# Two linear-attention and MLP layers on one core: entry sums, scalings, reciprocals and statistics rearranged

## The chip, the core and the metric

The kernel runs on one core of a Trainium2 chip. The core has five engines that run on their own and meet at semaphores: TensorE (PE; its weight loads are shown as PEld), VectorE (DVE), ScalarE (ACT), GpSimd (POOL) and SyncE (SP), which here issues all DMAs. The metric is the time of one execution on the device in microseconds. The kernel before takes 752.74 us (median of three runs, 752.65 to 752.99).

## The reference

The input x is 2048 rows of 576. Two blocks alternate, attention, MLP, attention, MLP, with the same weights both times, each behind a layer norm without gain, each added to x. Cut to what matters:

```python
q, k, v = ...                                # x @ wqkv, 32 heads of 18
phi = lambda t: where(t > 0, t + 1, exp(t)) + 1e-6
pq, pk = phi(q), phi(k)
kv  = einsum("bhsd,bhse->bhde", pk, v)       # per head, summed over all rows
z   = einsum("bhsd->bhd", pk)
num = einsum("bhqd,bhde->bhqe", pq, kv)
den = einsum("bhqd,bhd->bhq", pq, z)
x   = x + (num / den) @ wo
...
x   = x + gelu(layernorm(x) @ w1 + b1) @ w2 + b2    # 576 -> 4608 -> 576
```

## The kernel before

A row tile is 128 rows of x, so there are 16; a chunk is four row tiles. "Layer 0" and "layer 2" are the attentions, 1 and 3 the MLPs. The order of the work on each engine comes from three things: the order in which the program writes it, edges that only fix an order (`add_manual_dep` with NOSYNC; for TensorE they chain all its matmuls as written), and a planner at compile time that, where neither binds, puts on an engine what it reckons ready, the earlier written first. So ScalarE, VectorE and GpSimd may have an order other than the written one; each engine then runs its queue strictly in that order.

**Attention.** Instead of values, the kernel sums normalized rows against keys over all rows (`rows_by_keys`, matmuls L796) and multiplies the result by the value weights later (`kv_groups`, L849). Keys come in two halves of the heads. The first half's sums run during the row loop. The second half's are left for the entry, the stretch between the loop and the output stage: `sums(n)` does n row tiles of them, four matmuls of 0.12 us each (and one earlier for the tail). After the last one the sums are evicted to `k2` (`plus_eps`, L773 or L777), two by ScalarE and two by VectorE. Queries are projected feature group by feature group (`q_proj`, L718, L723) and passed through phi: an exponential (L640) and an identity (L644) on ScalarE, then L650 and the maximum L652 on VectorE. Four of the 18 query projections lie in the entry.

Denominators are computed for two chunks at a time (`den_stage`, L930; logarithm L934 and exponential L935 give reciprocals). `quad_stage` (L950) spreads the reciprocals of the last, small group of heads over a diagonal; `scale_stage` (L960, L962, L963) multiplies with them. For the four full groups `quarter_stage(c)` spreads them by 16 small matmuls (L974) into all four banks of the PSUM pool `ps_h` and ScalarE copies each bank out (L978); `quarter_scale(c, groups, after)` multiplies the queries in place on VectorE (L984), one instruction per group. `kv_groups` is masked on VectorE (L862) into block-diagonal `kvT`, and `kv_wo_half` (L878) multiplies it by half of the output weights. For the small group VectorE evicts (L881) and GpSimd copies the rows on (L884); the others are evicted by ScalarE or VectorE (L890). All of q, kv, kvwo, spread reciprocals and transposes share the four banks of `ps_h`, so a matmul that opens a bank waits for an eviction.

The output stage takes row tiles t = 0 to 15 in turn: ten matmuls (`wo_products`, L1121) into one of two other PSUM buffers, the residual sum on VectorE (L694), the store.

**Layer norm.** `LNPipe` carries each row tile through stages, one stage per `tick`: statistics (on VectorE L455, L456, L462 and L473 or L476; or on ScalarE in two passes, L429 for the mean and L442 for the squares, then L448 on GpSimd), the power -1/2 on GpSimd (L491), mean times that (L499), the normalization (L505 or L526 on GpSimd), and a transposition: by TensorE (L568) with a copy by ScalarE (L574), or by DMA from SyncE's queue (L552, L557), where it stands in one chain with the loads of the MLP's weights (L291). `hold` lets ticks pass first; `tp_at` is the output tile before which the transposition is not issued. In layer 0, `BY_ACT` names the input tiles whose statistics ScalarE takes; after each output stage the first four row tiles of the sum enter the pipe for the MLP.

## Time and profile before

The profiled execution took 753.01 us on the device; its span, from the first to the last instruction, is 751.3 us, at a granted TensorE clock of 1.00.

| stretch, us | what runs | PE busy | DVE busy | ACT busy | POOL busy |
|---|---|---|---|---|---|
| 0 to 20 | loads, first keys of layer 0 | 18.16 | 15.62 | 11.58 | 9.53 |
| 20 to 36 | layer 0, row loop | 15.63 | 12.32 | 12.11 | 13.38 |
| 36 to 55 | layer 0, row loop | 18.90 | 11.69 | 11.38 | 7.29 |
| 55 to 66 | layer 0, entry | 10.95 | 7.62 | 7.53 | 0.00 |
| 66 to 76 | layer 0, entry | 9.84 | 7.58 | 7.23 | 2.63 |
| 76 to 97 | layer 0, output stage | 21.00 | 17.41 | 10.84 | 9.15 |
| 378 to 424 | layer 2, row loop | 45.74 | 33.29 | 32.71 | 2.03 |
| 424 to 434 | layer 2, entry | 9.95 | 4.44 | 5.51 | 0.00 |
| 434 to 445 | layer 2, entry | 10.72 | 8.21 | 7.34 | 1.69 |
| 445 to 467 | layer 2, output stage | 21.49 | 16.60 | 12.40 | 8.64 |

The MLPs (97 to 378 and 467 to 751) keep TensorE busy throughout. A row of a timeline has the start in us, the time taken, the engine, the line, the operation, what it writes from what it reads, the shapes and the number of instructions merged; in brackets stands how long the engine idled before it and what ended that. A merged row can hide short waits, because the end of a matmul is modelled: the distance between starts shows them.

### The profile page before, as it was taken

The page shows a single profiled execution, that of the slowest core. Times are in us where ns is not written, and L with a number is a line of the kernel's source. Part 1 is how long each engine was busy: PE and PEld are TensorE (multiplying, and loading weights), DVE is VectorE, ACT ScalarE, POOL GpSimd, SP SyncE. Part 2 cuts the span into 40 slices and gives each one's busy share as a digit, 9 for nine tenths or more (in the row PEclk, how much of TensorE's full clock was granted, in tenths as well). Part 3 has the DMA queues.
Part 4 walks back from the last instruction along what each step waited for, and adds up shares of the span by engine and source line. Part 5 has one row for each costly group of instructions (what it writes and reads, how often), then busy time and mean ns, then how long its engine had stood idle before and what let it go on. Part 6 is the DMA issues. An engine that isn't in the chain of part 4 may idle for free.

```text
span 751.3 us, 15670 instructions
## 1 busy us (share of the span) xinstructions
PE 744.3 (99%) x6522; PEld 474.6 (63%) x6536; DVE 260.4 (35%) x645; ACT 314.8 (42%) x703; POOL 118.6 (16%) x220
## 2 busy tenths in 40 slices
PE   9999999999999999999999999999999999999998
PEld 5666744774576467547776666457646754774476
DVE  7767824235034404301367576500330041000000
ACT  5766656007501740363057665650263046105600
POOL 4831402003011201301000013300120020002000
PEclk9999999999999999999999999999999999999999
DMA  7797993027213701411404248420330033011000
GB/s 186 205 224 195 262 356 84 33 72 192 66 41 108 182 23 48 127 48 32 130 22 120 53 131 308 138 58 17 126 85 1 28 116 84 9 32 56 2 16 17
DMA packets 88545, 75.72 MB, mean 101 GB/s; under 512 B 45002, under 2 KB 73114, under 8 KB 88474
## 3 DMA queue, kind: packets, MB, share of 16 engines
q1 hardware_dynamic: 88474, 74.72, 35.0%
q8 instruction: 51, 0.84, 0.5%
q14 instruction: 20, 0.16, 0.1%
HBM read 48.10 MB, written 24.77 MB: 97 GB/s over the span
## 4 chain that ended last, share of the span: by engine, by line
PE 95%; DMA 2%; ACT 1%; SPq 1%; issue 1%; POOL 0%; DVE 0%; POOLq 0%
PE m_ps L1300 37%; PE h_ps L1236 21%; PE hp_ps L1236 17%; PE wo_ps L1121 5%; PE k_ps L751 4%; PE q_ps L718 4%; PE k_ps L796 4%; PE m_half L1300 1%; DMA wqkv_sb<-in_A_wqkv_dram 1%; PE q_ps L723 1%; DMA yT<-x 1%; PE k_tail L796 0%; PE rden_ps L974 0%; ACT turned L978 0%; PE kvwo_half L878 0%
## 5 line engine op out<-in xcount | busy, mean ns | idle before, releaser
L1300 PE MATMUL m_ps<-w_sb,hT 128*128 128x288 bf16 x2232 | 274.8, 286 | 0.0
L1300 PEld LDWEIGHTS <-hT 128*128 128x128 bf16 x2304 | 224.3, 98 | 60.4 <-issue 3.4
L1236 PEld LDWEIGHTS <-w_sb 64*128 64x128 bf16 x2304 | 124.6, 94 | 136.5 <-issue 1.9
L1236 PE MATMUL hp_ps<-yT,w_sb 64*128 64x512 bf16 x1152 | 178.0, 376 | 0.0
L1236 PE MATMUL h_ps<-yT,w_sb 64*128 64x512 bf16 x1152 | 147.9, 376 | 0.0
L1241 ACT COPY relay_sb<-relay_sb 128x1 f32<-128x1 f32 x144 | 28.5, 198 | 261.1 <-PE h_ps L1236 218.8
L1232 ACT ACTIVATE hT<-h_ps,b1T 128x512 bf16<-128x512 f32 x144 | 91.1, 683 | 44.4 <-PE h_ps L1236 44.4
L491 POOL TENSOR_TENSOR ln_rstd<-ln_u,neg_half 128x1 f32<-128x1 f32 x62 | 34.7, 561 | 367.2 <-DVE ln_u L473 213.1
L1232 ACT ACTIVATE hT<-hp_ps,b1T 128x512 bf16<-128x512 f32 x144 | 91.1, 692 | 0.0
L694 DVE TENSOR_TENSOR xbf<-m_ps,xo 128x576 bf16<-128x576 f32 x15 | 11.4, 758 | 213.5 <-PE m_ps L1300 213.5
L694 DVE TENSOR_TENSOR xo<-m_ps,xo 128x576 f32<-128x576 f32 x16 | 12.1, 758 | 167.8 <-PE m_ps L1300 167.8
L677 POOL TENSOR_TENSOR xo<-xo,b_bc 128x576 f32<-128x576 f32 x32 | 41.2, 1291 | 104.0 <-DMA xo<-x_d 91.4
L1236 PE MATMUL h_ps<-yT,w_tail 64*128 64x512 bf16 x144 | 54.1, 376 | 0.0
L1236 PE MATMUL hp_ps<-yT,w_tail 64*128 64x512 bf16 x144 | 54.1, 376 | 0.0
L751 PE MATMUL k_ps<-wqkv_sb,yT 128*128 128x288 bf16 (+1 forms) x320 | 44.5, 286 | 0.7 <-DMA wqkv_sb<-in_A_wqkv_dram 0.4
L1121 PE MATMUL wo_ps<-kvwo,pq 128*128 128x288 bf16 x320 | 42.3, 286 | 0.0
L718 PE MATMUL q_ps<-yT,wqkv_sb 128*128 128x512 bf16 x146 | 38.8, 379 | 0.7
L751 PEld LDWEIGHTS <-yT 128*128 128x128 bf16 x320 | 30.6, 97 | 11.8 <-DMA yT<-x 0.6
L1236 PEld LDWEIGHTS <-w_tail 64*128 64x128 bf16 x288 | 27.1, 94 | 17.1
L1121 PEld LDWEIGHTS <-pq 128*128 128x128 bf16 x320 | 30.6, 98 | 8.4 <-issue 0.3
L640 ACT ACTIVATE phi_e<-q_ps 128x512 bf16<-128x512 f32 (+1 forms) x38 | 21.6, 574 | 24.1 <-PE q_ps L718 21.1
L349 DVE STREAM_TRANSPOSE turned<-y_ring 128x576 bf16<-128x576 bf16 x40 | 30.4, 767 | 0.4
(161 smaller groups left out, 542.6 us busy)
## 6 DMA issues: line engine op xcount, KB each, us to landing
xo<-x_d SPq DMA_DIRECT2D x48, 288.0 KB
x_d<-xo SPq DMA_DIRECT2D x32, 288.0 KB
xl<-x_d SPq DMA_DIRECT2D x24, 288.0 KB
y_d<-turned SPq DMA_DIRECT2D x40, 144.0 KB
w_sb<-in_B_w_dram SPq DMA_DIRECT2D x6, 864.0 KB
yT<-y_d SPq DMA_DIRECT2D x10, 512.0 KB
w_sb<-in_B_w_dram SPq DMA_DIRECT2D x9, 512.0 KB
x_d<-xn SPq DMA_DIRECT2D x16, 288.0 KB
```

Of the source, the lines that this page charges most:

```text
L349: turn = nc.vector.transpose(out=turned[:, :, j, :], in_=y[:, 0:D])
L491: power = nc.gpsimd.tensor_tensor(out=rstd[:], in0=it["u"][:], in1=neg_half[:], op=ALU.pow)
L677: nc.gpsimd.tensor_tensor(out=xo[:], in0=xo[:], in1=b2_bc[:], op=ALU.add)
L694: total = nc.vector.tensor_tensor(out=xn[:, cols].rearrange("p (h n) -> p h n", h=2), in0=halves, in1=xo[:, cols].rearrange("p (h n) -> p ...
L718: pe(nc.tensor.matmul(qp[:], lhsT=wqkv_sb[:, k, g * P:(g + 1) * P], rhs=yT[:, k, c * CA:(c + 1) * CA], start=(k == 0), stop=(k == KD - 1)))
L751: pe(nc.tensor.matmul(kp[:, 0:n], lhsT=yT[:, k, t * P:(t + 1) * P], rhs=wqkv_sb[:, k, KH[half]:KH[half] + n], start=(k == 0), stop=(k == K ...
L796: pe(nc.tensor.matmul(dst, lhsT=lhsT, rhs=pk, start=(t == 0), stop=(t == NT - 1)))
L1121: pe(nc.tensor.matmul(wp[:, half, 0:HALF], lhsT=features, rhs=kvwo[slot][:, half * HALF:(half + 1) * HALF], start=(g == WO_ORDER[0]), stop ...
L1232: act_last["gelu"] = nc.scalar.activation(out=to, in_=ps, func=ACT.Gelu_apprx_tanh, bias=b1T[:, f:f + 1], scale=1.0).ins.name
L1236: mm = pe(nc.tensor.matmul(dst[n], lhsT=wt, rhs=mv, start=(seen[n] == 0), stop=(seen[n] == 8)))
L1241: relay = nc.scalar.copy(out=relay_sb[:, 1:2], in_=relay_sb[:, 0:1])
L1300: pe(nc.tensor.matmul(acc[half][:, 0:cols.stop - cols.start], lhsT=hT[f][:, j * P:(j + 1) * P], rhs=w2_sb[:, f, cols], start=(f == 0), sto ...
```

## The change

- Tile 10 of layer 0 leaves `BY_ACT`: VectorE takes its statistics. Its special ticks at t = 7 go.
- ScalarE takes the statistics of tile 3 of layer 0's sum (`t > 0` in place of `t in (1, 2)`). In layer 2, tile 2's second pass waits one tick more (`gap`) and is ordered behind the last scaling copy; for the input tiles the second pass loses its order edge.
- In the entry, a second row of sums stands ahead of `kv_wo_half(4, 0)`, and the query and the scalings of chunk 1 that stood in the middle go behind all sums and group 0's products. Scalings 0 and 1 follow there, ordered behind the eviction of the sums; scaling 2 behind the mask of groups 1 to 3; scaling 3 after output tile 1.
- `quad_stage(2)` runs on GpSimd after output tile 1, not on VectorE after tile 3.

```diff
-        BY_ACT = (10, 13)
+        BY_ACT = (13,)
...
-                        if it["t"] == BY_ACT[0] or it["kind"] == "B" and it["evac"] != "xbar":
-                            it["hold"] = int(it["kind"] == "A")
+                        if it["kind"] == "B" and it["evac"] != "xbar":
+                            it["hold"] = it["gap"]
                             continue
...
-                        if it["kind"] == "A":
-                            tc.add_manual_dep(two.ins, act_last["exp"], NOSYNC, reason="keys go on first")
+                        if it["gap"]:
+                            tc.add_manual_dep(two.ins, act_last["copy"], NOSYNC, reason="scalings first")
...
+                if engine is nc.vector:
+                    dve_last["k2"] = step.ins.name
...
-            def quad_stage(c, after=None):
+            def quad_stage(c):
...
-                    spread_out = nc.vector.tensor_tensor(
+                    spread_out = (nc.gpsimd if c else nc.vector).tensor_tensor(
...
-                    if t == 7:
-                        for _ in range(2):
-                            lnp.tick(transposes=0, only=BY_ACT[0])
...
             quarter_stage(1)
-            sums(1)
+            sums(2)
             kv_wo_half(4, 0)
             sums(1)
             kv_wo_half(4, 1)
-            quarter_scale(1, (0, 1, 2, 3), after=dve_last["quad"])
-            q_proj(*q_left.pop(0))
             sums(1)
             kv_wo_half(0, 0)
-            sums(1)
             kv_wo_half(0, 1)
+            quarter_scale(1, (0, 1), after=dve_last["k2"])
+            q_proj(*q_left.pop(0))
...
-                        hold, tp_at, by_act = ((2, 0, 4, 6)[t], (5, 7, 8, 12)[t], t in (1, 2))
+                        hold, tp_at, by_act = ((2, 0, 4, 6)[t], (5, 7, 8, 12)[t], t > 0)
...
             q_proj(*q_left.pop(0))
             kv_groups((1, 2, 3))
+            quarter_scale(1, (2,), after=dve_last["mask"])
             phi = q_proj(*q_left.pop(0), defer=True)
...
+                if t == 1:
+                    quarter_scale(1, (3,), after=total)
...
                 if t == 1:
                     den_stage(2)
-                if t == 3:
-                    quad_stage(2, after=total)
+                    quad_stage(2)
```

More of the change, by code (lines that the diff above doesn't have):

```diff
@@ L395, in __init__, with feed, tick @@
                 self.items = []
-            def feed(self, xt, t, kind, norm_eng, evac_eng="dve", load_from=None, after=None, hold=0, stats="dve", tp_at=0):
+            def feed(self, xt, t, kind, norm_eng, evac_eng="dve", load_from=None, after=None, hold=0, stats="dve", tp_at=0, gap=0):
                 self.items.append(dict(stage=(0 if load_from is None else -1), xt=xt, t=t, kind=kind,
                                        norm=norm_eng, evac=evac_eng, load=load_from,
-                                       after=after, hold=hold, stats=stats, tp_at=tp_at))
+                                       after=after, hold=hold, stats=stats, tp_at=tp_at, gap=gap))
             def busy(self):
                 return len(self.items)
-            def tick(self, transposes=1, only=None):
+            def tick(self, transposes=1):
                 land()
@@ L408, in tick @@
                     st = it["stage"]
-                    if only is not None and it["t"] != only:
-                        continue
                     if st == 4 and it["kind"] == "B" and it["evac"] == "xbar" and state["wo"] < it["tp_at"]:
@@ L865, in kv_groups @@
                     in1=maskz[0:126, :, :].unsqueeze(1).to_broadcast([126, n, 7, DH]), op=ALU.mult)
+                dve_last["mask"] = masked.ins.name
             def kv_wo_tiles():
@@ L945, in tile_of @@
                 return pq[(g, c - c % 2)][:, start:start + P], GF4 + j // 2
-            def quad_stage(c, after=None):
+            def quad_stage(c):
                 quad = blk.tile([P, D], BF16, name="quad_rden", tag="blk")
                 for i in range(2):
-                    spread_out = nc.vector.tensor_tensor(
+                    spread_out = (nc.gpsimd if c else nc.vector).tensor_tensor(
                         out=quad[:, 2 * i * P:2 * (i + 1) * P].rearrange("p (j n) -> p j n", j=2), in0=quad_mask[:],
                         in1=rden_of[c + i].unsqueeze(1).to_broadcast([P, 2, P]), op=ALU.mult)
-                    if after is not None:
-                        tc.add_manual_dep(spread_out.ins, after, NOSYNC, reason="sums first")
                 quad_rden[c] = quad
@@ L1130, in wo_stage @@
                     if li == 0:
-                        hold, tp_at, by_act = ((2, 0, 4, 6)[t], (5, 7, 8, 12)[t], t in (1, 2))
+                        hold, tp_at, by_act = ((2, 0, 4, 6)[t], (5, 7, 8, 12)[t], t > 0)
                     else:
                         hold, tp_at, by_act = ((2, 5, 8, 8)[t], (6, 9, 11, 13)[t], t in (1, 2))
-                    lnp.feed(xn, t, "B", "pool", "xbar" if li == 0 and t < 3 else "act", hold=hold, tp_at=tp_at,
+                    lnp.feed(xn, t, "B", "pool", "xbar" if li == 0 and t < 3 else "act", hold=hold, tp_at=tp_at, gap=int(li > 0 and t == 2),
                              **(dict(stats="act", after="rden") if by_act else dict(after="sum")))
```

2 lines of the change are left out of this document (1 added, 1 removed).

## The prediction

> **What bounds the kernel now.** I read the page first: engines, then the chain that ended last.
>
> ```profile
> PE 744.3 (99%) x6522; PEld 474.6 (63%) x6536; DVE 260.4 (35%) x645; ACT 314.8 (42%) x703; POOL 118.6 (16%) x220
> ...
> PE 95%; DMA 2%; ACT 1%; SPq 1%; issue 1%; POOL 0%; DVE 0%; POOLq 0%
> ```
>
> TensorE carries the time. No matmul is removed, so only moments in which TensorE waits can be won: 751.3 - 744.3 = 7.0 us, most of it ahead of 16 us, which no edit touches. The ends of matmuls are modelled, so I looked for waits by starts: a 288-column matmul follows the one before after 0.123 us and a 512-column one after 0.216. The timeline of TensorE at the two entries (71.27 is the first attention layer, "layer 0"; the rest is the second, "layer 2"):
>
> ```profile
> 434.23 0.66 PE L796 MATMUL k_ps<-pk,yrow_pair 128*128 128x288 bf16 x4
> 435.00 0.28 PE L878 MATMUL kvwo_half<-wo_sb,kvT 72*72 72x288 bf16 x1
> ...
> 439.21 1.45 PE L849 MATMUL kv_ps<-k,wqkv_sb 128*126 128x126 bf16 x15
> ...
> 71.27 1.02 PE L849 MATMUL kv_ps<-k,wqkv_sb 128*126 128x126 bf16 x15
> ...
> 448.43 0.40 PE L974 MATMUL rden_ps<-rden,head_bc 32*128 32x128 bf16 x16
> ...
> 454.26 0.23 PE L974 MATMUL rden_ps<-rden,head_bc 32*128 32x128 bf16 x3
> 455.01 0.38 PE L974 MATMUL rden_ps<-rden,head_bc 32*128 32x128 bf16 x13 [0.51 <-ACT yT L574]
> 455.32 0.91 PE L1121 MATMUL wo_ps<-kvwo,pq 128*128 128x288 bf16 x6
> ```
>
> See three waits. Four sums from 434.23 take 0.49, yet L878 starts at 435.00, not 434.73: 0.27. The same 15 matmuls of L849 take 1.45 in layer 2 and 1.02 in layer 0: 0.43. The 16 of L974 normally lead on after 0.33 (448.43 to 448.76), here after 1.06 (454.26 to 455.32): 0.72. ScalarE beside that last wait:
>
> ```profile
> 452.68 0.71 ACT L429 ACTIVATE ln_dump<-xo 128x576 bf16<-128x576 f32 x1
> ...
> 453.51 0.78 ACT L442 ACTIVATE ln_dump<-xo,ln_mv 128x576 bf16<-128x576 f32 x1
> 454.19 0.19 ACT L442 ACTIVATION_READ_ACCUMULATOR ln_dump<-xo,ln_mv 128x1 f32 x1
> 454.29 0.67 ACT L574 COPY yT<-tp 128x640 bf16<-128x640 bf16 x1
> 455.39 2.05 ACT L978 CAST turned<-rden_ps 128x512 bf16<-128x512 f32 x4 [0.43 <-PE rden_ps L974]
> 457.46 1.28 ACT L594 ACT_TABLE_LOAD   x1
> ```
>
> The copy that frees the bank (L574) stands behind both statistics passes of row tile 2. Last, the chain and GpSimd around 30 us:
>
> ```profile
> 31.19 4.16 DMA yT<-x
> ```
>
> ```profile
> 29.04 0.19 POOL L448 TENSOR_SCALAR ln_u<-ln_mv 128x1 f32<-128x1 f32 x1 [0.46 <-ACT ln_dump L442]
> ```
>
> Row tile 10's transposing DMA leaves at 31.19 and its keys start at 35.40; the five query matmuls before end at 34.06 + 5 x 0.216 = 35.14. Wait: 0.26.
>
> **The change part by part.** The sum is made against the profiled execution, 753.01 us (span 751.27 and 1.74 around it); that is 0.27 above the median 752.74, and I subtract the same sum from the median.
>
> *Tile 10 to VectorE (layer 0).* ScalarE loses two passes (0.69, 0.77), GpSimd one L448 (0.19); VectorE gains 0.45 + 0.44 + 0.21 + 0.15 = 1.25. VectorE waits 1.01 for exponentials ahead of 27.62, so about 0.25 of it pushes tile 7's key values; the sums that read them come a stage later (about 2.9 us). The power on GpSimd then waits no more for 29.23 but for tile 9's normalization (28.14) and at worst two mask steps (28.59): the DMA leaves about 0.7 earlier, more than the 0.26 it is late. SyncE's queue keeps its order; a weight piece behind it leaves earlier too. Gain 0.26; bounds 0 (if the landing does not follow the issue) and 0.26. Tile 13's passes lose an order edge only: 0.
>
> *Entry sums (both layers).* L878's product waits for a PSUM bank that ScalarE's first of four copies frees (434.95, start 435.00). One more row of sums, 0.49, ahead of it covers 0.27. The query after the second product also starts 0.09 late (435.61 to 435.82, where a product takes 0.12), behind VectorE's L881; it moves away. Gain 0.36 in each layer, 0.72 together. New: the last product of group 0 meets the fourth copy or the second L881, which I see end 0.15 before to 0.1 after it: cost 0 to 0.1 per layer, I take 0.
>
> *Keys' sums evicted earlier.* All sums now stand ahead of both queries. The evictions of the last ones (L773, 0.45 each, 0.81 for two) get 2 x 1.08 of query work more cover, less the moved sums; in layer 2 they also stand ahead of the scalings. The 0.43 goes; in layer 0 there is none. Gain 0.43.
>
> *Chunk 1's scalings in three places.* The same four instructions. Their price beside GpSimd copies:
>
> ```profile
> 68.51 1.43 DVE L984 TENSOR_TENSOR pq<-pq,turned 128x512 bf16<-128x512 bf16 x4
> ...
> 436.45 2.37 DVE L984 TENSOR_TENSOR pq<-pq,turned 128x512 bf16<-128x512 bf16 x4
> ```
>
> ```profile
> 436.45 1.75 POOL L884 COPY kvwo<-kvwo_rest 64x576 bf16<-64x576 bf16 x2 [34.04 <-DVE kvwo_rest L881]
> ```
>
> Alone four take 1.43, beside two copies 2.37: 0.47 more per copy. In layer 0 those copies come at 72.07 to 73.45 (they hang on a late bias load), and the third scaling now falls there, behind the mask (0.54) and a query's maximum (0.43). Queued behind it is L890's eviction of group 2; TensorE needs that bank 0.9 after its product and before had no slack (eviction over at 74.38, product at 74.45). I reckon the scaling ends 0.1 to 0.45 after the eviction is due: cost 0.2, bounds 0 and 0.45. The Trainium skill, page "SBUF — State Buffer", section "Who interferes with whom", states that a VectorE instruction with two SBUF inputs and a GpSimd instruction that reads SBUF block each other whole, first come first served. By that rule scaling and maximum would each wait out a copy of 0.66, the cost is the 0.45, and the sum is 0.25 smaller; the layer 2 rows (0.88 for a scaling that starts under a copy, 0.42 for the others) agree with it. In layer 2 the copies are over by about 438.4, before the third scaling: 0. The fourth, at tile 1, puts about 0.36 ahead of tile 2's sum; that ended at 448.20 and its bank is wanted at 448.76: 0, bounds 0 and 0.1. The scaled rows are used from tile 4 on.
>
> *Diagonal reciprocals on GpSimd.* VectorE loses 0.53 at 449.2, between sums that wait for TensorE: 0. No row shows this product on GpSimd. Below, 0.37 each (a 576-wide L526 at 0.82, by width); above, 1.29 each (L677's whole 576-wide product). By width L677 gives 0.57, two of them 1.15, which I take because it too has two inputs. From 446.9 they end at 448.1 (447.6 to 449.5); TensorE wants them at 450.00. Tile 0's power behind them moves from 447.56 to 448.15, and its row, finished at 449.84 before, is transposed at 452.67: 0 at either bound.
>
> *Statistics.* Layer 0, tile 3: VectorE loses 1.25 near 86, ScalarE, 52% busy there, gains 0.7 + 0.8: 0. Layer 2, tile 2: its second pass goes behind the next four copies. L574 then follows the first pass at 453.48, ends at 454.15, before the bank is wanted (454.33): gain 0.72. What is late next: on this clock the copies end at 456.75 and the second pass at 457.5. Meanwhile tile 3's statistics are ready at 456.29 (VectorE's last row, 456.13 + 0.15), and GpSimd would run its power, product and normalization (0.55 + 0.26 + 0.82, ending 458.2 with gaps). Tile 2's L448, L491, L499, L526, L536 (0.19 + 0.55 + 0.26 + 0.82 + 0.24, with gaps 2.5) then end at 460.7; TensorE wants tile 2's row after tile 11, at 460.51 - 0.69 = 459.82. Cost 0.7; if GpSimd keeps tile 2 first, its row ends at about 460.0 and the cost is at most 0.15. I take 0.7, since in time tile 3 is ready 1.2 earlier.
>
> Sum: 0.26 + 0.72 + 0.43 + 0.72 - 0.2 - 0.7 = 1.23 gained; 753.01 gives 751.78 and the median 751.5.
>
> **The rivals.** *Tile 2 first on GpSimd.* Before, its chain ran whole (455.49 to 457.99) though tile 3's input was ready at 456.29. For: it is written first. Against: then it was also ready first. Cost 0.15 instead of 0.7: gain 1.8, 750.9.
>
> *Second pass behind the table load (the slower side).* Before, the table load (1.28), its dummy (0.20) and tile 1's copy (0.67) come directly behind the four copies and hang on the same copy as the second pass now does. If they go first, the pass ends 2.1 later, at 459.9, tile 2's row at 462.4 and TensorE waits 2.3. This decides from 1.9 on (2.13 of gains less 0.2): 0.4 slower, 753.2. Against: the second pass is written six tiles earlier, and those three were merely all that was ready. The Trainium skill, "ScalarE: Activation LUTs", "Table sets: the hidden batching unit", counts cheap functions as part of every set, so the pass would need no load of its own; no run here shows a square under that table.
>
> *The waits do not go.* The written order is only a wish where nothing orders engines by an edge; the compiled order may put the copy behind other work, or tile 10's landing may not follow its issue. Without the 0.72 and the 0.26, but with the 0.7 lost: 0.25 gained, 752.5.
>
> **How the numbers follow.** About 0.2%, 1.5 us, is what a measurement tells from no change here: faster means below 751.2, slower above 754.2. Forecast 0.46, its own range 751.0 to 752.0 (layer 0's loss 0 to 0.45, banks 0 to 0.2, the 0.7 at 0.5 to 0.8); of it 0.13 lies below 751.2. Tile 2 first 0.25. Table load 0.10. Waits stay 0.08. A new wait that I have not seen 0.11, nearly all of it slower by over 0.2%. Faster 0.13 + 0.25 = 0.38; slower 0.11; same 0.51. The range 750.7 to 753.2 leaves out about 0.15.
>
> **What would show it.** L878 following its sums after 0.49; L849 at about 1.02 in layer 2; one unbroken row of 16 for L974 after tile 7; the key matmuls of tile 10 directly behind the queries. A wait of L568 before tile 2's transposes, released by GpSimd, of 0.7 (mine), under 0.2 (rival one) or over 1.9 (rival two). L878 of group 2 in layer 0 waiting for VectorE 0.2. Wrong would be any wait of TensorE over 0.3 elsewhere, above all for keys of tiles 11 to 15 or at the start of the MLP.

## The result, and the profile after

The kernel after takes 751.93 us (median of 22 runs, 751.45 to 752.73) beside 753.07 for the kernel before on the same chip (22 runs, 752.56 to 754.25): a ratio of 0.9985, 95% interval 0.9978 to 0.9992. Measured a second time, it took 751.94 beside 752.85, ratio 0.9989 (0.9980 to 0.9998). It is 0.9 to 1.1 us faster, about 0.1%: inside the 0.2% that the forecast called no change, and 0.4 above the 751.5 forecast.

The profiled execution took 752.26 us, with a span of 750.5 at a granted clock of 1.00. First the engines' row of the page of the kernel after.

```profile
PE 743.7 (99%) x6536; PEld 478.2 (64%) x6536; DVE 258.5 (34%) x641; ACT 314.9 (42%) x703; POOL 119.5 (16%) x224
```

TensorE does the same matmuls (their modelled busy time is 743.7 against 744.3), so only waits moved. Next the timeline of TensorE in the kernel after: start, time taken, engine, line, operation, shapes, number of instructions merged.

```profile
34.07 1.24 PE L716 MATMUL q_ps<-yT,wqkv_sb 128*128 128x512 bf16 x5
35.15 1.03 PE L749 MATMUL k_ps<-wqkv_sb,yT 128*128 128x289 bf16 x7
...
90.87 1.39 PE L1116 MATMUL wo_ps<-kvwo,pq 128*128 128x288 bf16 x10 [0.28 <-DVE xn L692]
...
433.96 1.15 PE L796 MATMUL k_ps<-pk,yrow_pair 128*128 128x288 bf16 x8
434.95 0.29 PE L879 MATMUL kvwo_half<-wo_sb,kvT 72*72 72x288 bf16 x1
...
438.59 1.02 PE L849 MATMUL kv_ps<-k,wqkv_sb 128*126 128x126 bf16 x15
...
453.21 0.40 PE L973 MATMUL rden_ps<-rden,head_bc 32*128 32x128 bf16 x16
453.55 2.62 PE L1116 MATMUL wo_ps<-kvwo,pq 128*128 128x288 bf16 x20
...
459.39 0.65 PE L566 MATMUL tp<-ident,y_ring 128*128 128x128 bf16 x5 [0.49 <-POOL y_ring L524]
...
465.15 1.04 PE L1233 MATMUL h_ps<-yT,w_sb 64*128 64x512 bf16 x8
466.03 0.38 PE L1233 MATMUL h_ps<-yT,w_tail 64*128 64x512 bf16 x1
466.22 0.62 PE L1233 MATMUL hp_ps<-yT,w_sb 64*128 64x512 bf16 x4
```

Read it against the rows of before. Won: the keys of tile 10 start at 35.15, five times 0.216 after the queries at 34.07. Eight sums from 433.96 take 0.99, and the first product follows at 434.95. The 15 matmuls of L849 take 1.02. The 16 of L973 are one row again, and the output matmuls follow after 0.34. Lost: a wait at 90.87 that before did not have at this size, the transposes of tile 2 in layer 2 at 459.39, and a step at the start of the last MLP. There the two 64-row halves of TensorE run beside each other; one of them should start its second block (`hp_ps`) at 466.03, and starts at 466.22.

To place every gain I compare the starts of TensorE's weight loads at equal points of the program. The executions reach the keys of tile 8 at 28.5 to 29.3 us; two executions of the kernel after differ by 0.29 there (29.09 and 28.80), so all shifts below are counted from that point. Minus is earlier than before. The column "after, again" is a second execution of the kernel after; those behind it are experiments, told further down.

```
                      before   after  after,  later   gap     later tp,  all three
                      us              again   tp      undone  stats back edits
keys of tile 15        50.05   -0.27  -0.27   -0.27   -0.27   -0.27      -0.08
layer 0, output 2      77.50   -0.54  -0.48   -0.54   -0.55   -0.53      -0.36
layer 0, output 12     90.87   -0.58  -0.52   -0.58   -0.58   -0.46      -0.28
layer 0, output 13     92.59   -0.28  -0.23   -0.29   -0.24   -0.35      -0.43
layer 2, entry done   445.87   -1.07  -1.01   -1.07   -1.02   -1.13      -1.22
layer 2, output 8     455.31   -1.79  -1.73   -1.79   -1.02   -1.85      -1.94
layer 2, output 13    461.89   -0.92  -0.87   -1.73   -1.02   -1.78      -1.87
last MLP starts       466.06   -0.92  -0.87   -1.69   -1.02   -1.85      -1.94
last MLP ends         747.63   -0.74  -0.44   -1.25   -1.02   -1.31      -1.71
```

So after: 0.27 (tile 10), 0.27 (entry of layer 0), 0.04, -0.30 (output tile 12 of layer 0), 0.79 (entry of layer 2), 0.72 (the bank of the spread reciprocals), -0.86 (tile 2's row), -0.19 (start of the last MLP): 0.74 in all. Both profiled executions of the kernel after lie 0.3 above its median (752.26 and 752.28), so their traces show somewhat less gain than the medians do. Three executions of the experiments were disturbed over their whole length (1,585 to 2,781 us) and are left out of the ratios; one of them is the profiled one of the kernel with tile 3's statistics alone put back, so nothing is read from its trace.

### The profile page after: what moved, and what is told of

It is laid out like the page before. It is cut to its first block, busy times and chain, and to the rows that moved or that the text cites. A ratio compares the mean times of both kernels' runs of the same rounds, so it can differ in the third digit from the quotient of the medians.

```text
span 750.5 us, 15681 instructions
## 1 busy us (share of the span) xinstructions
PE 743.7 (99%) x6536; PEld 478.2 (64%) x6536; DVE 258.5 (34%) x641; ACT 314.9 (42%) x703; POOL 119.5 (16%) x224
## 4 chain that ended last, share of the span: by engine, by line
PE 96%; DMA 1%; POOL 1%; ACT 1%; SPq 1%; issue 0%; DVE 0%; POOLq 0%
PE m_ps L1297 37%; PE h_ps L1233 20%; PE hp_ps L1233 17%; PE q_ps L716 4%; PE k_ps L749 4%; PE k_ps L796 4%; PE wo_ps L1116 4%; PE m_half L1297 1%; DMA wqkv_sb<-in_A_wqkv_dram 1%; PE q_ps L721 1%; PE k_tail L796 1%; DMA xo<-x_d 0%; PE kv_ps L849 0%; PE kvwo_half L879 0%; PE den_ps L931 0%; PE rden_ps L973 0%
## 5 line engine op out<-in xcount | busy, mean ns | idle before, releaser
L1233 PEld LDWEIGHTS <-w_sb 64*128 64x128 bf16 x2304 | 127.1, 94 | 133.0 <-issue 2.2
L1233 PE MATMUL hp_ps<-yT,w_sb 64*128 64x512 bf16 x1152 | 174.7, 376 | 0.0
L1233 PE MATMUL h_ps<-yT,w_sb 64*128 64x512 bf16 x1152 | 151.1, 376 | 0.0
L1238 ACT COPY relay_sb<-relay_sb 128x1 f32<-128x1 f32 x144 | 28.5, 198 | 261.2 <-PE h_ps L1233 218.7
```

The lines of the kernel that those rows point to most:

```text
L1233: mm = pe(nc.tensor.matmul(dst[n], lhsT=wt, rhs=mv, start=(seen[n] == 0), stop=(seen[n] == 8)))
L1238: relay = nc.scalar.copy(out=relay_sb[:, 1:2], in_=relay_sb[:, 0:1])
```

## Where the three losses sit in the profile after

ScalarE of the kernel after, around the moved statistics pass:

```profile
452.30 0.71 ACT L572 COPY yT<-tp 128x640 bf16<-128x640 bf16 x1
453.64 2.05 ACT L977 CAST turned<-rden_ps 128x512 bf16<-128x512 f32 x4 [0.63 <-PE rden_ps L973]
455.56 0.81 ACT L440 ACTIVATE ln_dump<-xo,ln_mv 128x576 bf16<-128x576 f32 x1
...
456.47 1.28 ACT L592 ACT_TABLE_LOAD   x1
```

The copy that frees the bank is done at 453.02, before the bank is wanted, as forecast. The second pass goes directly behind the four copies and ahead of the table load, so the forecast's second rival does not happen. Its results reach GpSimd at 456.5. GpSimd of the kernel after, with the reciprocals' product, the rows of layer 0 and those of layer 2:

```profile
88.04 0.55 POOL L497 TENSOR_SCALAR ln_nmr<-ln_mv,ln_rstd 128x1 f32<-128x1 f32 x1
88.69 0.82 POOL L524 TENSOR_SCALAR y_ring<-xn,ln_rstd,ln_nmr 128x576 bf16<-128x576 f32 x1
...
445.99 1.29 POOL L951 TENSOR_TENSOR quad_rden<-quad_mask,rden 128x256 bf16<-128x256 bf16 x2 [8.20 <-issue]
...
456.82 0.55 POOL L489 TENSOR_TENSOR ln_rstd<-ln_u,neg_half 128x1 f32<-128x1 f32 x1
457.47 0.54 POOL L497 TENSOR_SCALAR ln_nmr<-ln_mv,ln_rstd 128x1 f32<-128x1 f32 x1
457.98 0.54 POOL L489 TENSOR_TENSOR ln_rstd<-ln_u,neg_half 128x1 f32<-128x1 f32 x1
458.52 0.82 POOL L524 TENSOR_SCALAR y_ring<-xo,ln_rstd,ln_nmr 128x576 bf16<-128x576 f32 x1
459.32 0.26 POOL L497 TENSOR_SCALAR ln_nmr<-ln_mv,ln_rstd 128x1 f32<-128x1 f32 x1
```

In layer 2 the order is power 2, mean 2, power 3, normalization 2, mean 3. Of tile 3's work only the power (0.54) stands ahead of tile 2's normalization: the compiled order interleaves the two tiles. Then 0.28 more goes to the multiplication of the mean at 457.47, which takes 0.54 where it takes 0.26 undisturbed (459.32). VectorE of the kernel after shows what lay beside it:

```profile
89.04 1.11 DVE L983 TENSOR_TENSOR pq<-pq,turned 128x512 bf16<-128x512 bf16 x2
...
457.13 0.75 DVE L983 TENSOR_TENSOR pq<-pq,turned 128x512 bf16<-128x512 bf16 x2
...
465.41 0.76 DVE L692 TENSOR_TENSOR xo<-wo_ps,xo 128x576 f32<-128x576 f32 x1 [2.12 <-DMA xo<-x_d]
```

At 457.13 two scalings run back to back, and GpSimd's small instruction, which starts at 457.47, ends only at 458.01. In layer 0 it is the other way round: GpSimd's normalization starts at 88.69, the third scaling meets it at 89.04, and the two scalings take 1.11 where two take 0.75; the residual sum behind them and with it output tile 12 are late. The same two instructions in the kernel before, GpSimd, then VectorE:

```profile
88.75 0.99 POOL L526 TENSOR_SCALAR y_ring<-xn,ln_rstd,ln_nmr 128x576 bf16<-128x576 f32 x1 [0.31 <-DMA yT<-y_ring]
```

```profile
89.63 0.78 DVE L984 TENSOR_TENSOR pq<-pq,turned 128x512 bf16<-128x512 bf16 x2
```

There the normalization started 0.89 ahead of the third scaling, and that scaling took 0.41. In after the scalings, which follow TensorE, come 0.59 earlier, the normalization only 0.06: it starts 0.35 ahead, and the two meet.

The third row of VectorE above is the loss at the last MLP: the sum of output tile 14, whose end frees the bank for `hp_ps`, stood idle for 2.12 waiting for its input row from memory ("row 14" below). In before it waited for that row too. VectorE, then TensorE, of the kernel before:

```profile
465.70 0.76 DVE L694 TENSOR_TENSOR xo<-wo_ps,xo 128x576 f32<-128x576 f32 x1 [1.51 <-DMA xo<-x_d]
```

```profile
466.94 1.24 PE L1236 MATMUL hp_ps<-yT,w_sb 64*128 64x512 bf16 x8
```

The sum ended at 466.46, 0.48 before TensorE wanted its bank.

## Experiments

Two theories stood at the start on where the gains go. The ledger: each of TensorE's waits counts in full until something else is late. The row-14 theory: the start of the last MLP is tied to the landing of one input row, so gains before it can be lost there. And three causes were weighed for the wait at output tile 12 of layer 0: tile 3's statistics, against the reciprocals' product on GpSimd, against TensorE's lead alone.

**Tile 2's transposes one output tile later.** On the kernel after:

```diff
-                        hold, tp_at, by_act = ((2, 5, 8, 8)[t], (6, 9, 11, 13)[t], t in (1, 2))
+                        hold, tp_at, by_act = ((2, 5, 8, 8)[t], (6, 9, 12, 13)[t], t in (1, 2))
```

> One change to the kernel after: the transposes of tile 2 in layer 2 go behind output tile 12 instead of tile 11, so 1.23 us more of TensorE work covers the row that GpSimd finishes at 459.34. The ledger theory (each wait of TensorE counts in full until something else is late): the 0.86 wait goes and the kernel is 0.86 faster than after, 2.0 faster than before. The row-14 theory (in after the lower half of TensorE starts its second block of the last MLP 0.19 late because the bank of output tile 14 is freed by a residual sum, and that sum waits until 465.30 for its input row): TensorE arrives 0.86 earlier, but the sum still ends near 466.17, so the lower half waits about 1.05 instead of 0.19, and the end moves by 0 to 0.1 only: 1.1 to 1.3 faster than before.

Measured: 751.78 beside 752.88 before, ratio 0.9984 (0.9975 to 0.9993), so in time not to be told from after. The trace (column "later tp") tells more. The wait of 0.86 is gone, output 13 stands at -1.73; but at the end only -1.25 is left. Of the 0.86 a part of 0.51 came through, between the two theories. Small waits of 0.11 follow at the last output tile, and the half of TensorE waits 0.44 for `hp_ps` instead of 0.19. So the ledger is wrong by what row 14 takes; the row-14 theory was wrong in holding the row's landing fixed: the sum of tile 14 began 0.5 earlier than in after, counted from the keys of tile 8.

**The first MLP group in other banks.** On the kernel after; the second line shows the same with the later transposes.

```diff
+                if c == 0 and g == 0:
+                    hps = [ps_h.tile([P, 512], F32, name="h_ps", tag="h") for _ in range(4)]
+                    dst = [hps[0][:], hps[2][:], hps[1][:], hps[3][:]]
+                elif c == 0 and g == 1:
+                    pairs = [ps_acc.tile([P, 2, 512], F32, name="hp_ps", tag=next_acc()) for _ in range(2)]
+                    dst = [pairs[0][:, 0, :], pairs[1][:, 0, :], pairs[0][:, 1, :], pairs[1][:, 1, :]]
+                else:
```

> One change to the kernel after: the first group of four blocks in each MLP's first chunk takes four banks of ps_h, the second group takes both output buffers; from the third on all is as it was. No block of the first group then waits for a residual sum. If the 0.19 in after is the bank of output tile 14, it goes and the end is 0.19 earlier than in after; in layer 0 nothing changes. If the 0.19 comes from elsewhere (the transposed rows, the relay between the halves), it stays. A loss of up to 0.6 if the second or third group now waits for an eviction.

> Both edits on the kernel after: tile 2's transposes behind output tile 12 and the first group of the MLP in ps_h. The row-14 theory: now the whole 0.86 + 0.19 = 1.05 shows, 2.2 faster than before, though either edit alone gives at most 0.2. The ledger theory without the bank: 0.86 with or without the second edit, so the two kernels with the later transposes end within 0.2 of each other.

Measured: 753.78 (ratio 1.0011, 1.0002 to 1.0021) and 753.17 (1.0006, 0.9997 to 1.0015) beside 752.88. Both are slower than after. In both traces the step at the start of the MLP is gone, and a new wait stands in the second group, in both MLPs; TensorE of the kernel with the banks alone:

```profile
471.70 1.03 PE L1240 MATMUL hp_ps<-yT,w_sb 64*128 64x512 bf16 x8
473.50 0.37 PE L1240 MATMUL hp_ps<-yT,w_tail 64*128 64x512 bf16 x1 [0.78 <-ACT hT L1236]
```

The releaser that the profile names is ScalarE's eviction of the group's first block. I read it so that a matmul writing one bank of a pair waits for the eviction of the other; no run here tests that. From start to start (472.35 to 473.50, less 0.22) the wait is 0.94, and there is one in each MLP. As a remedy the edit is therefore of no use, but it does show that the step hangs on the bank. VectorE, then TensorE, of the kernel with both edits:

```profile
466.56 0.76 DVE L692 TENSOR_TENSOR xo<-wo_ps,xo 128x576 f32<-128x576 f32 x1 [2.02 <-DMA xo<-x_d]
```

```profile
466.79 1.24 PE L1240 MATMUL h_ps<-yT,w_sb 64*128 64x512 bf16 x8
```

The sum of tile 14 ends at 467.31 here, 0.53 after TensorE reached the second block, and that block, now in another bank, starts at 466.79 all the same. In this kernel the output matmuls of tile 15 also wait, 1.06 at 464.59, behind the sum of tile 13, the load of whose row left 2.1 later than in after.

**Tile 3's statistics of layer 0 back on VectorE**, alone and with the later transposes:

```diff
-                        hold, tp_at, by_act = ((2, 0, 4, 6)[t], (5, 7, 8, 12)[t], t > 0)
+                        hold, tp_at, by_act = ((2, 0, 4, 6)[t], (5, 7, 8, 12)[t], t in (1, 2))
```

> One part of the change undone: in layer 0 the statistics of tile 3 are on VectorE again, which also takes one step off GpSimd. In after TensorE waits 0.30 more than before at output tile 12 of layer 0, behind a scaling on VectorE of 0.74 that starts beside GpSimd's normalization of tile 3. If the extra step on GpSimd (0.19 to 0.24) and ScalarE's later finish have moved that normalization under the scaling, the wait goes back to 0 to 0.05 and the first MLP starts 0.3 earlier than in after. If it is the product of the diagonal reciprocals on GpSimd, or the query side's earlier start alone, that moved it, the 0.30 stays.

> Tile 2's transposes in layer 2 behind output tile 12, and tile 3's statistics in layer 0 back on VectorE. If the extra step on GpSimd and the later finish of ScalarE made the wait of 0.30 at output tile 12 of layer 0, TensorE starts output tile 13 there 0.56 ahead of before instead of 0.27 and the first MLP with it; if the diagonal reciprocals on GpSimd made it, 0.27 stays. In layer 2 as in the kernel with the transposes moved alone. With both, 1.6 to 1.9 faster than before, against 1.1 for after.

Measured: alone 751.79 beside 752.88 (0.9985, 0.9976 to 0.9994). With the later transposes 751.34 beside 752.89, ratio 0.9981 (0.9972 to 0.9989). In that trace output tile 12 of layer 0 waits 0.12 more than before instead of 0.30, but 0.11 is lost at output tile 9, where the statistics on VectorE stand between sums. Net 0.07. Neither expectation (0.30 back, or nothing) came true. GpSimd, then VectorE, of that trace:

```profile
88.53 0.82 POOL L524 TENSOR_SCALAR y_ring<-xn,ln_rstd,ln_nmr 128x576 bf16<-128x576 f32 x1
```

```profile
88.96 1.04 DVE L983 TENSOR_TENSOR pq<-pq,turned 128x512 bf16<-128x512 bf16 x2
```

The third scaling still meets the normalization, 0.43 after its start, and takes 0.66 (0.74 in after). So the moved statistics made this collision worse; they did not make it.

**The reciprocals' product back on VectorE**, on the kernel after:

```diff
-                    spread_out = (nc.gpsimd if c else nc.vector).tensor_tensor(
+                    spread_out = nc.vector.tensor_tensor(
```

> One part of the change undone: the product of the last four heads' reciprocals with the diagonal mask is on VectorE again, after output tile 1. The forecast costs the move at 0 in both layers: nothing on TensorE changes, within 0.05, in layer 2. In layer 0, if the 1.3 of that product on GpSimd is what pushed the normalization of tile 3 under VectorE's scaling, the wait of 0.30 at output tile 12 goes; if it is tile 3's own statistics, it stays.

Measured: 751.80 beside 752.89 (0.9987, 0.9978 to 0.9996). The wait at output tile 12 of layer 0 stays, with 0.26: the product is not its cause. Layer 2 gains and loses up to output tile 13 as in after (0.78, 0.72, -0.86). The last MLP starts without its step in this trace: the sum of tile 14 began 1.05 earlier than in after, with the same order of loads and stores on SyncE's queue in layer 2. The row's landing is thus not a constant of the kernel.

**The kernel after once more.**

> The kernel after, unchanged, profiled a second time: which of the small waits belong to the kernel and which to the one execution. The wait ahead of tile 2's transposes in layer 2 (0.86) and the gains of 0.72, 0.79 and 0.27 stay within 0.05. The wait at output tile 12 of layer 0, if it follows from the moved statistics of tile 3, stays between 0.25 and 0.35. The loss at the start of the last MLP follows the landing of row 14, which moved by up to 0.5 between runs of the same code around it: 0 to 0.3. The end 0.6 to 0.8 ahead of before, counted from the keys of tile 8.

Measured: 751.94 (ratio above). The waits at 459 (0.86) and at output tile 12 of layer 0 (0.29) and the gains of 0.72 and 0.79 repeat to 0.01. The entry of layer 0 gains 0.21 instead of 0.27, and the step at the last MLP is 0.42 instead of 0.19; both are outside what was expected (0 to 0.3, and an end 0.6 to 0.8 ahead): the end is only 0.44 ahead. VectorE, and in a second fence TensorE, of this second execution:

```profile
465.41 0.76 DVE L692 TENSOR_TENSOR xo<-wo_ps,xo 128x576 f32<-128x576 f32 x1 [2.32 <-DMA xo<-x_d]
```

```profile
464.92 1.04 PE L1233 MATMUL h_ps<-yT,w_sb 64*128 64x512 bf16 x8
...
466.22 1.04 PE L1233 MATMUL hp_ps<-yT,w_sb 64*128 64x512 bf16 x8
```

`hp_ps` starts 0.05 after the sum's end, 466.17, while the first block had begun at 464.92 and lasts 0.88 in the half that goes on first. That gives a rule to test on every trace: the step is the sum's start + 0.76 + 0.05 - (MLP's start + 0.88), or 0. It gives 0.19 in after, 0.43 here, 0.44 with the later transposes, 0.54 with tile 3's statistics back besides, and 0 in before and with the product on VectorE. The measured steps are 0.19, 0.42, 0.44, 0.54, 0 and 0. This rule, and the kernel with the other banks, in which the step is gone though the sum ended late, tie the end to row 14.

**The moved pass put back** (layer 2, tile 2), on the kernel after:

```diff
-                    lnp.feed(xn, t, "B", "pool", "xbar" if li == 0 and t < 3 else "act", hold=hold, tp_at=tp_at, gap=int(li > 0 and t == 2),
+                    lnp.feed(xn, t, "B", "pool", "xbar" if li == 0 and t < 3 else "act", hold=hold, tp_at=tp_at, gap=0,
```

> One part of the change undone: tile 2's second statistics pass in layer 2 stands where it stood, ahead of the copies of the spread reciprocals. The forecast's working (0.72 against 0.7) and the trace of after (0.72 against 0.86) both say that this part is worth about nothing: the wait of the spreading matmuls after tile 7 returns with 0.72, the wait ahead of tile 2's transposes goes with 0.86, so output tile 12 of layer 2 starts 0.14 earlier than in after. From there on the end gains 0 to 0.2, because the sum of tile 14 waits for its input row. The rival, that the move of this pass is what made layer 2 faster: the end is 0.5 to 0.7 later than in after.

Measured: 751.47 beside 752.89, ratio 0.9981 (0.9972 to 0.9990). TensorE in layer 2:

```profile
452.72 0.23 PE L973 MATMUL rden_ps<-rden,head_bc 32*128 32x128 bf16 x3
453.47 0.38 PE L973 MATMUL rden_ps<-rden,head_bc 32*128 32x128 bf16 x13 [0.52 <-ACT yT L572]
...
458.97 0.44 PE L566 MATMUL tp<-ident,y_ring 128*128 128x128 bf16 x5
```

The wait after tile 7 is back and the one ahead of the transposes is gone: output 13 stands at -1.02 against -0.92 in after, 0.1 earlier. And this order also has no step at the MLP, for it arrives there no earlier than the row: -1.02 at the end, 0.28 better than the one execution of after and 0.57 better than the other. So the part of the change that won its 0.72 exactly as forecast is, taken whole, a small loss in these traces: 0.14 within layer 2 up to output 13 against both executions of after, the rest by the landing of row 14. By time alone that is not shown (1.42 faster than before, against 1.14 and 0.91, with overlapping intervals). The rival, which had it as what made layer 2 faster, falls.

**Rows asked for one tile later**, with the later transposes:

```diff
-                if li == 0 and t + AHEAD + 2 < NT or 0 < t < NT - AHEAD - 1 and li > 0:
-                    prefetch_xo(li, t + AHEAD + (1 if li > 0 else 2), add_b2=False)
+                if li == 0 and t + AHEAD + 2 < NT or 1 < t < NT - AHEAD and li > 0:
+                    prefetch_xo(li, t + AHEAD + (0 if li > 0 else 2), add_b2=False)
```

> The later transposes again, and in layer 2 each input row is asked for one output tile later (four ahead instead of five). On SyncE's queue the load that waits for the normalization of tile 1 then has one store more ahead of it, and the stores are not all held up behind it; the wait of 2.3 for a store to complete before the load of a later row gets shorter or goes. If that queue order is what makes the row of tile 14 land late, the sum of tile 14 starts right behind its matmuls and the lower half of TensorE loses under 0.05 at the start of the last MLP instead of 0.23: 0.2 to 0.4 earlier at the end than with the later transposes alone. If the transfers themselves are the limit (the DMA engines are nearly full from 455 to 468), or if loads one tile later come too late, the lower half loses as much or more, and sums of tiles 12 to 15 wait for their rows by up to 1.

Measured: 751.72 beside 752.89 (0.9983, 0.9974 to 0.9992). The step grows to 0.74 (the rule gives 0.74):

```profile
464.22 1.04 PE L1233 MATMUL h_ps<-yT,w_sb 64*128 64x512 bf16 x8
...
465.84 1.04 PE L1233 MATMUL hp_ps<-yT,w_sb 64*128 64x512 bf16 x8 [0.37 <-DVE xo L692]
```

One load changed places with a store on SyncE's queue, and the sum of tile 14 begins 0.37 later than with the later transposes alone, not earlier. In this one trace the shuffle of the queue is no remedy; that loads came too late remains possible beside it.

**Tile 1's statistics earlier.** What holds SyncE up is the load of tile 10's row: its buffer comes free only when GpSimd has normalized tile 1, at 454.05, and the queue stands from 451.7. So this kernel has the later transposes, tile 3's statistics on VectorE, and in layer 2:

```diff
-                        hold, tp_at, by_act = ((2, 5, 8, 8)[t], (6, 9, 12, 13)[t], t in (1, 2))
+                        hold, tp_at, by_act = ((2, 3, 8, 8)[t], (6, 9, 12, 13)[t], t in (1, 2))
```

> The kernel with the later transposes and tile 3's statistics of layer 0 on VectorE, and one more edit: in layer 2 the statistics of tile 1 go two ticks earlier, ahead of the four copies near 448, so GpSimd normalizes tile 1 near 451 instead of 454.0. SyncE's queue then isn't held up from 451.7 to 454.0 by the load whose buffer that normalization frees, and the DMA engines don't stand idle from 453 to 455. If that standstill is why the row of tile 14 lands only 4.6 to 5.7 after its load was issued, the row lands 1 or more earlier, sums 13 to 15 follow their matmuls at once, and the 0.54 that the kernel without this edit loses between output tile 8 and the end of the last MLP goes: 2.0 faster than before. If the landing hangs on the transfers behind it or on the store that the load of tile 13 waits for, it moves by under 0.3 and the end by under 0.1: 1.5 faster than before.

Measured: 751.09 beside 752.76, ratio 0.9979 (0.9970 to 0.9987). SyncE's queue, first of the kernel after, then of this one:

```profile
454.07 0.80 SPq L668 DMA_DIRECT2D xo<-x_d  x2
```

```profile
451.91 0.32 SPq L668 DMA_DIRECT2D xo<-x_d  x1
```

And the busy times by stretch, after and then this kernel; the last two columns are the share of the DMA engines' time and GB/s.

```profile
453.00:459.00 6.00, 5.90 (x64) 4.34 (x61) 5.28 (x14) 4.90 (x10) 3.45 (x8) 1.00 0.66 209
459.00:466.00 7.00, 6.58 (x58) 4.80 (x60) 2.80 (x4) 1.38 (x2) 1.79 (x5) 1.00 0.99 355
```

```profile
453.00:459.00 6.00, 6.00 (x66) 4.73 (x65) 5.55 (x14) 4.88 (x9) 2.30 (x5) 1.00 0.91 278
459.00:466.00 7.00, 7.00 (x66) 4.87 (x66) 2.97 (x5) 1.58 (x3) 1.76 (x5) 1.00 0.95 300
```

The load leaves 2.2 earlier, and the transfers that were crowded behind 459 (0.99 busy, 355 GB/s) are spread: 278 and 300. TensorE, by its modelled ends, is busy without a break from 453 to 466. The sum of tile 14 begins 0.4 earlier than in the kernel without this edit, the step falls from 0.54 to 0.23 (the rule: 0.23), and between output 8 and the end 0.22 is lost instead of 0.54. The row came 0.4 earlier, not the 1 or more that was expected. That the standstill is a part of the cause fits this, but is not shown: between traces with one and the same queue order that start moved by up to 1.05.

The trace puts this kernel 0.97 and 1.27 ahead of the two executions of after, though 0.19 of the tile-10 gain did not come in it. The medians agree in sign (1.67 faster than before, after 1.14 and 0.91), but the intervals overlap; by time alone it is not proven better than after.

In this kernel, too, layer 0 behaves otherwise than in the one with the same code there: output tile 12 waits 0.15 less than before. GpSimd and VectorE of it:

```profile
89.30 1.37 POOL L524 TENSOR_SCALAR y_ring<-xn,ln_rstd,ln_nmr 128x576 bf16<-128x576 f32 x1 [0.53 <-DMA yT<-y_ring]
```

```profile
89.31 0.75 DVE L983 TENSOR_TENSOR pq<-pq,turned 128x512 bf16<-128x512 bf16 x2
```

Here a DMA held the normalization back to 89.30, and GpSimd paid (1.37 against 0.82) where TensorE does not wait for it; the two scalings took their usual 0.75. Over all traces with the change's layer 0, output tile 12 waits 0.26 to 0.34 more than before in the eight that have tile 3's statistics on ScalarE (0.30 and 0.29 in after), and 0.12 and -0.15 in the two that have them on VectorE. In the second of these two the DMA decided, so what the statistics cost rests on the first alone.

**Two parts of the change alone**, on the kernel before: the entry (its part of the diff in the front), and `BY_ACT = (13,)` with the special ticks gone.

> The kernel before with the entry alone changed: the second row of sums ahead of the first product, the query behind all sums, the scalings of chunk 1 in three places. By the trace of after: 0.27 in layer 0 (0.36 less 0.09) and 0.79 in layer 2 (0.36 and 0.43) gained; the wait of 0.72 after tile 7 of layer 2 stays. The wait at output tile 12 of layer 0: if it comes from TensorE's lead over a GpSimd that is no earlier, it shows here too, with 0.15 to 0.3; if it comes from the moved statistics of tile 3, nothing shows here. In all 1.06 gained without it, 0.76 to 0.9 with it.

> The kernel before with tile 10's statistics on VectorE and nothing else. The keys of tile 10 follow the queries without a wait: 0.26 gained, kept to the end. If TensorE's lead alone makes the new wait at output tile 12 of layer 0, a part of the 0.26 is lost there.

Measured: 751.82 beside 752.76 (0.9987, 0.9977 to 0.9996), and 752.50 (0.9996, 0.9987 to 1.0005). Tile 10 alone gives 0.27 at the keys and 0.07 more at two small waits of layer 0's output stage. Nothing is lost at output tile 12, which TensorE reaches 0.31 earlier than in before; but a DMA holds the normalization back there too, to 89.66, behind the start of the third scaling (89.52). The entry alone gives 0.79 in layer 2, as in after, and nothing at all in layer 0: 0.36 is won at the products and 0.35 lost again ahead of the next ones. It does not have the wait at output tile 12 either, but it has no lead: TensorE comes there 0.14 later than in before. So neither run decides whether TensorE's lead makes that wait. TensorE, GpSimd and VectorE of the entry alone in layer 0:

```profile
73.14 0.58 PE L881 MATMUL kvwo_half<-wo_sb,kvT 126*126 126x288 bf16 x3 [0.19 <-DVE kvT L864]
```

```profile
70.97 1.51 POOL L887 COPY kvwo<-kvwo_rest 64x576 bf16<-64x576 bf16 x2
```

```profile
71.88 0.75 DVE L650 TENSOR_SCALAR phi_e<-phi_e 128x512 bf16<-128x512 bf16 x1
72.55 0.53 DVE L864 TENSOR_TENSOR kvT<-kv_ps,maskz 126x378 bf16<-126x378 f32 x1
```

GpSimd's copies run from 70.97 to 72.48 here. The query's steps on VectorE in front of the mask take 0.75 and 0.69 (0.28 and 0.42 in after, where the copies were over at 70.62), the mask is late, and TensorE waits 0.26 for it. The third scaling runs in 0.41 at 73.00, free of the copies. All traces with this entry also lose 0.09 at the last product of group 2. ScalarE's evictions of the products, in the kernel after:

```profile
73.19 0.70 ACT L891 CAST kvwo<-kvwo_half 126x288 bf16<-126x288 f32 x2 [1.24 <-PE kvwo_half L879]
```

That product waits for the second of these, over at 73.89, and starts at 73.94. In before it waited for VectorE's eviction, in front of which the third scaling now stands; in after that one is over at 73.77, in time. So the 0.09 is not a wait for the scaling.

## Why the prediction was right, and where it was not

The time came within the range, and the medians' gain of 1.14 and 0.91 is near the 1.23 that was forecast. That nearness is in part luck: the traces have 0.74 in one execution and 0.44 in the other, because two losses that the sum did not have (0.30 and 0.19 to 0.42) came on top of gains that were right; what the executions near the median lose there no trace shows. Point by point:

- **Tile 10: 0.26.** Measured 0.27, alone and in after. The landing followed the issue.
- **Entry sums: 0.36 per layer. Keys' sums evicted earlier: 0.43 in layer 2.** Both right: 0.36 in layer 0 ahead of its loss, 0.79 together in layer 2, in the part alone as in after.
- **Layer 0's loss: 0.2, bounds 0 and 0.45.** Measured 0.08 in after, 0.14 in its second execution, 0.35 in the entry alone. That the size lay within the bounds is luck, for the mechanism was not the one named. No trace shows TensorE waiting behind the third scaling: the steady 0.09 is a wait for ScalarE's eviction. The rest, 0 to 0.26, comes when the copies slow the query's steps ahead of the mask, and when they come hangs on a bias load: their first starts at 69.04, 70.41 and 70.97 in three executions and at 72.07 in before. I had taken that 72.07 for a property of the kernel. The page of the Trainium skill that the forecast weighed ("SBUF — State Buffer", "Who interferes with whom") has the two engines block each other, first come first served; by it scaling and maximum would each wait out a copy. In the two traces with copies around the scaling it took 0.42 and 0.46, so it waited out no whole copy. In one of them (the later transposes, copies from 71.47 to 72.98) the query's maximum behind it took 0.88 against 0.42, which agrees, and TensorE lost no more than the 0.09 in either.
- **Spread reciprocals: 0.72.** Right to 0.01, one row of 16.
- **New wait for tile 2's transposes: 0.7.** Measured 0.86 in three traces and 0.87 in a fourth, in all that have the moved pass and not the later transposes. The size was near, the working was not: I let GpSimd run all of tile 3 (power, product, normalization) ahead of tile 2. In the trace tile 3's power alone is ahead (0.54), and two scalings on VectorE hold up tile 2's mean by 0.28. Rival one, tile 2 first, was half right in this; a planner interleaved the two chains, which neither I nor the rival had.
- **Reciprocals on GpSimd: 0.** Right; each took 0.67 where I had 0.57, and with the product back on VectorE no wait of 0.05 or more appears or goes in layer 2's output stage ahead of the last MLP.
- **Statistics of tile 3 in layer 0: 0.** This step failed: output tile 12 waits 0.30 more. I counted what VectorE loses and ScalarE gains and asked neither what GpSimd does more (the row L446) nor when its chain then ends. Relative to TensorE the normalization came 0.5 later than before and met a scaling. With the edit undone and no DMA in the way, 0.18 of the 0.30 went at this tile, but 0.11 was lost at tile 9, so 0.07 was left at the end of layer 0; the other trace with the edit undone kept 0.34 (both counted from the keys of tile 15), because there a DMA held the normalization back. The larger part of the wait is thus not the statistics'. The sum has no term for what is left: scalings that follow TensorE's gain of 0.58 while GpSimd's chain does not. The product of the reciprocals is ruled out as its cause (0.26 without it); that TensorE's lead is the cause is my reading of the rows, and no run shows it by itself.
- **Unforeseen: the step at the start of the last MLP, 0.19 and 0.42.** I had named a wait there, over 0.3, as a sign of being wrong, and the second execution has one, but I had not priced it. The slack of 0.48 in before was to be read from the trace: with the row where it was, every gain in layer 2 beyond half a microsecond goes into it. Beside the 0.86, it is why 0.72 + 0.79 of gain could not be added up to the end.
- **Where TensorE's 7.0 us of idle time lie.** Not mostly ahead of 16 us, as the forecast read it: 1.84 of them do, and 3.3 lie behind the last matmul (747.96 to 751.27). No edit touches either, so the sum does not change.

The rival "table load" (slower; its 753.2 should be 753.1, 752.74 and 0.4) did not occur, and the waits that should go went. Whether a square needs a table load of its own stays unseen: the pass ran ahead of the load. The pass without its move, 0.28 to 0.57 better at the end of the traces than with it, shows that the change contained a step that, taken alone, forecast and trace both call a wash or worse.

What stays open: why row 14 takes 4.1 to 5.8 us from its load's issue to the start of its sum, with 1.1 us between traces that have the same order on SyncE's queue there (4.7 and 5.8). The transfers crowd (0.99 busy), and in the one trace in which they are spread the row came 0.4 earlier, which is less than that scatter. Open, too, is what makes the larger part of the wait at output tile 12 of layer 0.

## What to carry to other kernels

Before adding gains up, look at the next point that does not move with the engine that gains: here an input row from memory with half a microsecond of slack to the bank that its sum frees. Count a moved step on every engine that its chain passes through, and when the last of them will now run beside something else. And a time that hangs on a DMA, read from one execution, is a sample: in a second execution of the same kernel the sum that waits for row 14 began 0.29 later, counted from the keys of tile 8, and GpSimd's copies behind the bias load began at 70.41 in place of 69.04.

## What was not expected of the hardware

- An instruction of GpSimd on 128x1 elements takes 0.26 alone and 0.54 to 0.66 beside two back-to-back scalings of VectorE; a normalization 0.82 alone and 1.37 behind them; a scaling 0.42 alone and 0.74 when the normalization was there first; and VectorE's `tensor_scalar` on 128x512 bf16, with one input, 0.28 alone and 0.69 to 0.78 beside GpSimd's copies. Which of the two engines pays cannot be told from the recorded starts alone: with GpSimd 0.35 ahead (88.69 against 89.04) VectorE paid 0.33, with GpSimd 0.01 ahead (89.30 against 89.31) GpSimd paid 0.55. The Trainium skill, "SBUF — State Buffer", "Who interferes with whom", has this as an exclusive lock in order of issue. The traces agree that one of them waits; the order of issue they do not show.
- A bank that comes late holds up one 64-row half of TensorE by itself: in after the other half ran on with its own block (466.03) and stayed 0.19 ahead through the first chunk of the MLP. From the next matmuls over all rows on, both were 0.19 late. In the second execution the step is 0.42, and the other half was only 0.19 ahead of the late one: it lost the rest itself.
